# Other written lists of operations for the five engines of an attention and two-layer feed-forward kernel

## The chip, the core and the metric

The kernel runs on one core of a Trainium2 chip. TensorE (PE) multiplies matrices, VectorE (DVE), ScalarE (ACT) and GpSimd (POOL) work elementwise, SyncE (SP) only issues transfers, and 16 DMA engines carry them. PEld is TensorE's weight load, which runs beside its matmuls. The metric is the device time of one launch in microseconds (us), as the median of several runs; lower is better.

## The reference, cut to what matters

```python
# attention: 2 batches x 8 heads, 768 rows of 64; proj is 64 x 6
q_bits = einsum('bhsd,dk->bhsk', q, proj) > 0          # the same for k
mask = q_bucket[..., :, None] == k_bucket[..., None, :]   # 6 bits make a bucket
scores = where(mask, q @ k.T / sqrt(64), -1e9)
attn = exp(scores - scores.max(-1)); attn /= attn.sum(-1) + 1e-9
x = (attn @ v), heads side by side                     # 1536 x 512
# layer 1
h = x @ w_in                                           # 512 -> 2048
x = (h - tanh(h)) @ w_out                              # 2048 -> 512
# layer 2
g = x @ w_gate; val = x @ w_val                        # 512 -> 1536, twice
out = (g * sigmoid(g) * val) @ w_out2                  # 1536 -> 512
```

The weights of the two layers arrive as 64-bit floats and are turned into 32-bit ones on the chip.

## The kernel before, in words

**Attention.** The 16 heads are done as 8 pairs, numbered 0 to 7. A pair is 12 steps (96 in all, steps 0 to 95, so pair 4 begins with step 48): half of the queries, head of the pair, and one of three blocks of 128 query rows. A step is: a score product on PE (four matmuls, L746), a row maximum on DVE (L756), an exponential on ACT (L758), a reciprocal of the sum (L762 and L764), a scaling of the 128x768 block on POOL (L765), six transposes on PE (L776), and two copies out of PSUM on ACT or DVE (L782). Every six steps PE multiplies the transposed block with v (L799).

**Operands of a pair.** For each pair but the first, SP loads both heads of q and of k as 128x768 (L651, into `fs`). Each is split in a high and a low part: the high part by POOL or ACT (L570 or L568), the low part by DVE (L666). The parts are written to the buffers `f` and `q` (high and low part of q) and to the two halves of `raw` (high and low part of k); the names are by turns. From there SP moves them by DMA, SBUF to SBUF, into the operands `op` of the score products: 18 moves for each of seven pairs (L656, 126 in all), 96 KB for a move from `f` or `q` and 192 KB for one from `raw`. A buffer can be written again when the moves out of it have landed, so the split of the next pair waits for the moves of this one. PE also hashes the pair's heads (L709, then bits on DVE, L609, and one-hot products, L743), which DVE and ACT place in the operands (L680, L698). Pair 0 is prepared on its own (L625, L603, L568 to L597) without moves.

**Feed-forward.** From about 241 us PE runs the products of the two layers (L955 and L1009), for which SP loads weights (L371), DVE converts them, and ACT and POOL split them (L385, L387).

**What sets the order.** Every operation has a number, given when it is declared. A planner (`Plan.order`) gives each engine its instructions: the table `ORDER` holds one list of numbers for each of PE, DVE, ACT, POOL and SP, and as long as a list lasts, the engine takes exactly the next number on it. Where an operation may run on two engines, the list in which it stands decides. After its list's end an engine takes the earliest due operation. The program is then written in that order, and on the chip each engine runs its instructions strictly one after the other: one that waits holds up all that stand behind it on that engine. SP is such an engine too, so a move that waits for its source or for its place holds up every later load and move.

Of the kernel before, what the change touches and what calls it, by code (L numbers as in the profile page):

```python
# [46 lines left out]
def chunk_keys():  # L47
# [5 lines left out]
    for i in range(NP2):  # L53
# [11 lines left out]

ORDER = {e: [int(n) for n in t.split()] for e, t in dict(
    PE="""
# [15 lines left out]
    """,  # L83
    DVE="""
# [18 lines left out]
    """,  # L103
    ACT="""
# [15 lines left out]
    """,  # L120
    POOL="""
# [9 lines left out]
    """,  # L131
    SP="""
# [7 lines left out]
    """,  # L140
).items()}

# [1056 lines left out]
```

## Time and profile before

| what | value |
|---|---|
| median of 3 runs | 785.4 us (784.09 to 789.57) |
| the profiled execution | 785.25 us |
| its span, first to last instruction | 783.1 us |
| granted TensorE clock | 1.000 over the span |
| PE busy | 756.5 us (97%) |
| PEld busy | 663.4 us (85%) |
| DVE, ACT, POOL busy | 603.0, 475.5, 333.0 us |

The profiled execution stands 0.15 us under the median. Busy time of PE is counted from modelled ends of pipelined matmuls. A table of stretches (further down) shows where in the span each engine is busy; a wait in brackets behind a row is idle time of that row's engine and what ended it.

### The profile page before, as it was taken

How to read it: one execution, taken by the hardware profiler on the slowest of the kernel's cores; microseconds unless marked ns; L12 is line 12 of the kernel's file. 1: busy time of each engine (PE TensorE's matmuls, PEld its weight loads, DVE VectorE, ACT ScalarE, POOL GpSimd, SP SyncE). 2: the span in 40 equal slices, each digit the busy share in tenths (PEclk: the TensorE clock that was granted, in tenths of full speed). 3: DMA queues.
4: the chain of work that ended last, by engine and by line, in shares of the span. 5: the costliest groups of instructions: out<-in, count | busy, mean ns of one | idle time of the engine just before them, and what ended most of it. 6: DMA issues, size and time to landing. Idle time of an engine off the chain costs nothing.

```text
span 783.1 us, 12379 instructions
## 1 busy us (share of the span) xinstructions
PE 756.5 (97%) x4332; PEld 663.4 (85%) x4332; DVE 603.0 (77%) x1097; ACT 475.5 (61%) x974; POOL 333.0 (43%) x353
## 2 busy tenths in 40 slices
PE   5899999899999999999999999999999999999998
PEld 2667666677678899999999999989998998989996
DVE  4878777668988985988687789898896966777355
ACT  3877777688887664656555656665554554555430
POOL 2655567856776822314232333534332441422120
PEclk9999999999999999999999999999999999999999
DMA  4655361665422132787676671433537657754675
GB/s 128 175 144 152 87 172 40 154 148 159 134 83 82 55 95 65 169 194 196 148 194 151 159 165 57 106 108 109 183 94 177 137 129 156 154 108 75 122 166 197
DMA packets 38717, 104.23 MB, mean 133 GB/s; under 512 B 4704, under 2 KB 10080, under 8 KB 38656
## 3 DMA queue, kind: packets, MB, share of 16 engines
q1 hardware_dynamic: 28288, 71.06, 29.5%
q0 software_dynamic: 9904, 31.59, 23.5%
q10 hardware_dynamic: 464, 0.80, 0.4%
q8 instruction: 34, 0.56, 0.3%
q14 instruction: 27, 0.22, 0.1%
HBM read 49.17 MB, written 18.87 MB: 87 GB/s over the span
## 4 chain that ended last, share of the span: by engine, by line
PE 84%; DMA 7%; DVE 5%; issue 1%; POOL 1%; ACT 1%; SPq 1%; ACTq 0%; DVEq 0%; POOLq 0%
PE bs L955 30%; PE t L1009 15%; PE h L1009 8%; PE s L746 7%; PE x L799 6%; PE t L776 6%; PE x L1009 5%; DMA raw<-in_w 2%; PE x L955 2%; DMA fs<-in_kT 2%; PE t L955 2%; DMA op<-f 1%; DVE m L756 1%; PE h L955 1%; POOL ct L765 1%
## 5 line engine op out<-in xcount | busy, mean ns | idle before, releaser
L955 PE MATMUL bs<-x,wi 128*128 128x384 f32 x1200 | 233.3, 335 | 3.2 <-DVE ct L938 3.2
L955 PEld LDWEIGHTS bs<-x,wi 128*128 128x128 f32 x1200 | 210.3, 188 | 10.5 <-DVE ct L938 5.3
L765 POOL TENSOR_SCALAR ct<-ct,r 128x768 f32<-128x768 f32 x96 | 92.9, 972 | 45.6 <-DVE r L764 31.0
L756 DVE TENSOR_REDUCE m<-s 128x1 f32<-128x768 f32 x96 | 91.1, 952 | 12.7 <-PE s L746 10.5
L746 PE MATMUL s<-op 128*128 128x384 f32 x384 | 94.8, 370 | 2.9 <-ACT ct L758 1.3
L758 ACT ACTIVATE ct<-s,m 128x768 f32<-128x768 f32 x96 | 86.4, 901 | 13.2 <-DVE m L756 9.1
L776 PEld LDWEIGHTS t<-csb,ct 128*128 128x128 f32 x576 | 66.5, 140 | 30.0 <-POOL ct L765 11.2
L776 PE MATMUL t<-csb,ct 128*128 128x128 f32 x576 | 84.2, 276 | 7.9 <-POOL ct L765 6.3
L935 ACT ACTIVATE ct<-bs 128x384 f32<-128x384 f32 x120 | 58.7, 490 | 48.9 <-PE bs L955 48.6
L782 ACT ACTIVATE pt<-t 128x384 f32<-128x384 f32 x129 | 60.6, 489 | 36.9 <-PE t L776 34.8
L746 PEld LDWEIGHTS s<-op 128*128 128x128 f32 x384 | 65.6, 194 | 14.8 <-ACT ct L758 7.0
L1009 PE MATMUL t<-op,wo 128*128 128x384 f32 x384 | 76.5, 335 | 0.0
L799 PE MATMUL x<-pt,v 128*64 128x384 f32 x384 | 69.0, 495 | 0.0
L1009 PEld LDWEIGHTS t<-op,wo 128*128 128x128 f32 x384 | 67.2, 188 | 0.8 <-DVE op L872 0.4
L1009 PE MATMUL t<-wo,op 128*128 128x512 f32 x264 | 67.8, 393 | 0.0
L387 POOL TENSOR_TENSOR wi<-fs,wi 128x512 fp32r<-128x512 f32 (+1 forms) x26 | 40.1, 1544 | 57.0 <-ACT wi L385 56.9
L872 POOL TENSOR_TENSOR ct<-ct 128x384 f32<-128x384 f32 x22 | 23.0, 1045 | 82.4 <-ACT ct L891 62.4
L1009 PEld LDWEIGHTS t<-wo,op 128*128 128x128 f32 x264 | 48.9, 187 | 7.9
L1046 POOL DMA_DIRECT2D acc<-ct x24 | 21.1, 877 | 72.5 <-ACT ct L1038 29.6
L385 ACT ACTIVATE wi<-fs 128x512 fp32r<-128x512 f32 (+1 forms) x60 | 41.8, 701 | 14.1 <-PE bs L955 4.0
L799 PEld LDWEIGHTS x<-pt,v 128*64 128x64 f32 x384 | 24.7, 136 | 28.6 <-issue 28.1
L955 PE MATMUL bs<-op,wi 128*128 128x384 f32 x240 | 47.5, 335 | 0.0
(166 smaller groups left out, 1382.9 us busy)
## 6 DMA issues: line engine op xcount, KB each, us to landing
raw<-in_w SPq DMA_DIRECT2D x68, 512.0 KB, 4.1
acc<-ct POOLq DMA_DIRECT2D x24, 768.0 KB, 6.1
out<-acc POOLq DMA_DIRECT2D x16, 768.0 KB, 7.5
op<-raw SPq DMA_DIRECT2D x42, 192.0 KB, 3.5
op<-f SPq DMA_DIRECT2D x56, 96.0 KB, 3.8
v<-in_v SPq DMA_DIRECT2D x8, 384.0 KB, 4.4
out<-acc SPq DMA_DIRECT2D x4, 768.0 KB, 3.8
acc<-out SPq DMA_DIRECT2D x4, 768.0 KB, 4.4
```

Of the source, the lines that this page charges most:

```text
L385: op({"ACT": act(n)}, lambda e: e.activation(out=hi, in_=src, func=ACTF.Copy), r=rk, w=[wk + (0,)], due=due, late=late)
L387: op({"POOL": pool(n), "DVE": dve(n)}, lambda e: e.tensor_tensor(out=lo, in0=src, in1=hi.bitcast(F32), op=ALU.subtract), r=rk + [wk + (0,) ...
L746: g.matmul(out=s[:, kh, 0:TB], lhsT=(b, a)[first][:, q0], rhs=ks[kh][0 if first else 1], start=first, stop=not first,)
L756: op({"DVE": 0.87}, lambda g: g.tensor_reduce(out=m, in_=sv, axis=AX.XY, op=ALU.max, negate=True), r=[sk + (0,), sk + (1,)], w=[mk])
L758: op({"ACT": 0.9}, lambda g: g.activation(out=p.rearrange("p (a b) -> p a b", a=2), in_=sv, func=ACTF.Exp, bias=m, accum_out=sm), r=[sk + ...
L765: op({"POOL": 0.91}, lambda g: g.tensor_scalar(out=p, in0=p, scalar1=r, scalar2=1.0, op0=ALU.mult, op1=ALU.mult), r=[pk, rk], w=[pk])
L776: g.transpose(out=t_t[z][:, kt * 128:(kt + 1) * 128], in_=p[:, z * TB + kt * 128:z * TB + (kt + 1) * 128], identity=ident)
L782: g.activation(out=dst, in_=src, func=ACTF.Copy) if g is nc.scalar else g.tensor_copy(dst, src),
L799: g.matmul(out=x[r, :], lhsT=v[:, kt, r], rhs=pt_t[ptks[e][1]][:, kt, :], start=(kt == 0), stop=(kt == NKT - 1), tile_position=(0, 64 * e),)
L935: op({"ACT": act(TB)}, lambda e: e.activation(out=dst, in_=bank(), func=ACTF.Copy), r=[bk], w=dk, due=due)
L955: e.matmul(out=bank(), lhsT=w[:, wpart, wi * 256 + k * 128:wi * 256 + k * 128 + 128], rhs=x_at(sb, xn, xpart, k), start=first and m == 0, ...
L1009: e.matmul(out=ps(), lhsT=lhs, rhs=rhs, start=c == 0, stop=c == 5)
```

## The change

The five lists of `ORDER` are other lists. They hold the same operations, and no other line of the kernel differs: the same loads, moves, splits, tiles and buffers. Some 110 operations of the attention stand on another engine than before: 62 of the 192 copies out of PSUM, half of them each way between ACT and DVE, 34 of the small additions (L762) between DVE and POOL, and 15 splits and preparations between ACT and POOL. Of the 14 splits into a high part ACT had three (q of pair 1, k of pairs 2 and 4) and now has five (k of pairs 1 and 7, q of pairs 2, 4 and 7); POOL has the rest. The ends of the lists are alike (PE's from the last steps of the attention on, DVE's and POOL's also), so what moves lies in the attention. Of the diff, the first line of two lists:

```diff
     PE="""
-        13 28 24 20 15 54 64 33 74 40 48 35 44 84 100 102 62 60 112 70 72 135 80 82 145 90 92 157 108 110 167
...
+        13 28 24 20 15 33 54 44 48 64 40 35 74 100 84 62 60 102 72 70 112 135 80 82 145 92 90 157 110 108 167
...
     SP="""
-        5 6 10 9 94 95 123 183 211 127 53 179 181 122 126 261 182 178 207 209 124 128 205 260 177 289 210 293
...
+        5 6 10 9 95 94 53 126 123 128 261 181 179 127 122 124 177 178 206 209 182 183 205 219 289 260 288 211
...
```

Three places show what moves. The first is DVE at the very start, where `bits` is the hash of pair 0's heads (`h` the first, `x` the second head), `m` the row maximum of a step, and `op` the operands. Before:

```order
L579 SCALAR_TENSOR_TENSOR op<-f,op 64x384
L583 TENSOR_SCALAR op<-t,csb 64x384
L756 TENSOR_REDUCE m<-s_116 128x1
L579 SCALAR_TENSOR_TENSOR op<-q,op 64x384
L756 TENSOR_REDUCE m<-s_112 128x1
L609 TENSOR_SCALAR bits<-x 128x384
L594 TENSOR_TENSOR op<-raw,op 64x384 x2
L583 TENSOR_SCALAR op<-h,csb 64x384
L756 TENSOR_REDUCE m<-s_116 128x1
```

and after:

```order
L583 TENSOR_SCALAR op<-t,csb 64x384 x2
L609 TENSOR_SCALAR bits<-x 128x384
L594 TENSOR_TENSOR op<-raw,op 64x384
L756 TENSOR_REDUCE m<-s_116 128x1
L579 SCALAR_TENSOR_TENSOR op<-q,op 64x384
L756 TENSOR_REDUCE m<-s_112 128x1
L583 TENSOR_SCALAR op<-h,csb 64x384
L764 RECIPROCAL r<-r 128x1
L594 TENSOR_TENSOR op<-raw,op 64x384
L756 TENSOR_REDUCE m<-s_116 128x1
```

The second head's bits and one of its two subtractions (L594) now stand ahead of the first maximum, and one split (L579) that stood there is put off. On PE the second head's hash likewise stands ahead of the first score product, where it stood behind the second.

The second place is SP at pair 4's moves and pair 5's loads. Of these rows `raw` is a move of k, `f` and `q` one of the high and of the low part of q, `in_qT` and `in_kT` the loads of pair 5, and `v` the load of v. Before:

```order
L656 DMA op<-raw 64x768
L656 DMA op<-q 64x384
L656 DMA op<-raw 64x768
L656 DMA op<-f 64x384 x2
L656 DMA op<-q 64x384
L656 DMA op<-f 64x384 x3
L787 DMA v<-in_v 128x768
L656 DMA op<-raw 64x768
L651 DMA fs<-in_qT 128x768
L651 DMA fs<-in_kT 128x768
```

and after:

```order
L656 DMA op<-raw 64x768
L787 DMA v<-in_v 128x768
L656 DMA op<-raw 64x768
L656 DMA op<-f 64x384
L656 DMA op<-q 64x384
L656 DMA op<-raw 64x768 x3
L651 DMA fs<-in_kT 128x768
L656 DMA op<-raw 64x768
L656 DMA op<-f 64x384
L656 DMA op<-q 64x384 x2
L651 DMA fs<-in_qT 128x768
```

The move of the low part of q, which stood second, stands behind two moves of k, the load of v and one move of the high part of q; the loads of pair 5 are parted, k's first, behind five of the six moves of k (the sixth follows directly), and q's last.

The third place is POOL at the splits of pair 5, where `raw<-fs` is the high part of k, `f<-fs` that of q, and L765 the scaling of a step. Before:

```order
L570 TENSOR_SCALAR raw<-fs 128x768
L765 TENSOR_SCALAR ct<-ct,r 128x768
L570 TENSOR_SCALAR f<-fs 128x768
L765 TENSOR_SCALAR ct<-ct,r 128x768
L762 TENSOR_SCALAR r<-sm 128x1
```

and after:

```order
L570 TENSOR_SCALAR raw<-fs 128x768
L765 TENSOR_SCALAR ct<-ct,r 128x768
L463 TENSOR_TENSOR x_58<-ct,x_58 128x384
L765 TENSOR_SCALAR ct<-ct,r 128x768 x2
L468 TENSOR_TENSOR ct<-ct 128x384
L765 TENSOR_SCALAR ct<-ct,r 128x768
L468 TENSOR_TENSOR ct<-ct 128x384
L570 TENSOR_SCALAR f<-fs 128x768
```

The split of k stands behind the same scaling as before, the split of q three scalings later.

## Rows read from the trace of the kernel before

**Rows 1.** Busy time in stretches: stretch, its length, then busy us of each engine.

```profile
0.00:22.00 22.00, 12.47 (x51) 6.63 (x52) 11.99 (x24) 9.58 (x17) 6.30 (x15) 1.00 0.44 114
22.00:40.00 18.00, 14.69 (x96) 11.21 (x95) 14.98 (x30) 15.60 (x33) 12.51 (x20) 1.00 0.75 201
40.00:114.00 74.00, 73.16 (x482) 52.09 (x484) 58.56 (x118) 57.94 (x126) 43.40 (x61) 1.00 0.54 141
114.00:122.00 8.00, 4.91 (x32) 3.30 (x30) 3.93 (x6) 3.98 (x9) 6.07 (x7) 1.00 0.13 32
122.00:145.00 23.00, 23.00 (x152) 16.05 (x150) 16.89 (x40) 19.53 (x45) 14.87 (x20) 1.00 0.47 119
145.00:150.00 5.00, 2.90 (x21) 1.77 (x18) 2.11 (x5) 2.19 (x5) 4.57 (x7) 1.00 0.66 128
150.00:241.00 91.00, 90.67 (x586) 63.79 (x585) 77.77 (x160) 72.68 (x158) 63.27 (x78) 1.00 0.44 123
241.00:783.10 542.10, 534.73 (x2928) 508.57 (x2926) 416.79 (x720) 294.05 (x585) 181.98 (x151) 1.00 0.56 134
```

**Rows 2.** Who PE waited for, 22 to 241 us: total, times, longest.

```profile
PE t L776 <- POOL ct L765: 6.3, 7, 1.8
...
PE s L746 <- DMA op<-f: 1.0, 1, 1.0
```

**Rows 3.** POOL in order of time: start, length, instruction, idle before it.

```profile
114.94 0.83 POOL L570 TENSOR_SCALAR raw<-fs 128x768 fp32r<-128x768 f32 x1 [4.15 <-DMA op<-raw]
115.75 0.90 POOL L765 TENSOR_SCALAR ct<-ct,r 128x768 f32<-128x768 f32 x1
117.20 0.95 POOL L570 TENSOR_SCALAR f<-fs 128x768 fp32r<-128x768 f32 x1 [0.54 <-DMA op<-f]
...
144.25 0.83 POOL L570 TENSOR_SCALAR raw<-fs 128x768 fp32r<-128x768 f32 x1 [1.63 <-DMA op<-raw]
```

**Rows 4.** The chain of waits that ended last: start, length, what held.

```profile
35.80 3.83 DMA op<-f
...
105.67 8.40 DMA fs<-in_kT
...
125.25 0.70 PE s L746 x4
...
142.79 4.99 DMA op<-q
```

**Rows 5.** SP's queue in order of time, as it issues transfers.

```profile
87.80 0.46 SPq L656 DMA_DIRECT2D op<-raw  x1
98.84 0.46 SPq L656 DMA_DIRECT2D op<-q  x1
...
114.13 0.61 SPq L656 DMA_DIRECT2D op<-f  x1
133.14 0.46 SPq L656 DMA_DIRECT2D op<-q  x1
```

**Rows 6.** DMA issues: queue, count, size, median us from issue to landing.

```profile
op<-raw SPq DMA_DIRECT2D x42, 192.0 KB, 3.5
```

**Rows 7.** DVE in order of time at the start.

```profile
14.97 0.96 DVE L756 TENSOR_REDUCE m<-s 128x1 f32<-128x768 f32 x1
16.14 0.56 DVE L609 TENSOR_SCALAR bits<-x 128x384 bf16<-128x384 f32 x1 [0.21 <-PE x L625]
16.73 1.02 DVE L594 TENSOR_TENSOR op<-raw,op 64x384 fp32r<-64x384 f32 x2
18.68 0.62 DVE L583 TENSOR_SCALAR op<-h,csb 64x384 fp32r<-64x384 f32 x1 [0.93 <-PE h L603]
19.33 0.96 DVE L756 TENSOR_REDUCE m<-s 128x1 f32<-128x768 f32 x1
...
20.91 0.22 DVE L764 RECIPROCAL r<-r 128x1 f32<-128x1 f32 x2
```

**Rows 8.** DVE in order of time at the splits of pair 6.

```profile
147.89 1.12 DVE L666 SCALAR_TENSOR_TENSOR raw<-fs,raw 128x768 fp32r<-128x768 f32 x1 [3.08 <-DMA op<-q]
```

124 rows, old and new, of tables (ACT, DVE, PE, POOL) are left out of this document.

## The prediction, made blind

> **What bounds the kernel now.** I read the table of stretches first [rows 1]. From 150 us on PE is the bound: it is busy for 90.67 of 91.00 us up to 241 us and for 534.73 of 542.10 us behind that. In the attention it is not busy for 9.53 us of the first 22, 3.31 us of the next 18, 0.84 us from 40 to 114, 3.09 us from 114 to 122, nothing up to 145, and 2.10 us from 145 to 150. The same operations stand in the new lists, so PE's own work stays, and what a new order can give is in these gaps: 9.67 us between 22 and 241 us, and a part of the first 22. Behind 241 us the lists are nearly alike, so I expect the rest to start earlier or later as a whole.
>
> Then who PE waited for [rows 2]: mostly transposes that wait for POOL's scaling, 6.3 us in seven waits, and one score product that waits for a move, 1.0 us. POOL in order of time says why the scaling is late [rows 3]: at 114.94 it starts the split of pair 5's k after 4.15 idle us that a landing move of `raw` ended. It had come there at 110.79 (114.94 - 4.15), and the scalings of the running steps stood behind the split. The split of q at 117.20 waits again, 0.54 us, for a move of `f`. At 144.25 it is the same with pair 6: 1.63 us.
>
> Last, why the moves land late. The chain of waits has a load of k that takes 8.40 us from issue to landing at 105.67, and a move that takes 4.99 us at 142.79 [rows 4], against a median of 3.5 us for the moves of k [rows 6]. SP's queue shows what came ahead of them [rows 5]: it issues a move of pair 4 at 87.80, and nothing more until 98.84, since the next number on its list is a move of a low part that DVE had not made yet. From 98.84 to 114.13 the rest of pair 4, the load of v and both loads of pair 5 go out in one bunch. Then SP stands again until 133.14, for a place of pair 5 that a running step still reads, and a second bunch follows; the split of pair 6 waits for that one.
>
> **The change part by part.**
>
> *Start.* Between the starts of the second maximum, 14.97, and the third, 19.33, DVE spends 4.36 us [rows 7]. In the new list four things stand from the one to the other: the maximum (0.96), the placing L583 (0.62), a reciprocal (0.11, half of two) and one subtraction L594 (0.51, half of two), together 2.20 us; the idle 0.21 and 0.93 us go, because the second head is hashed earlier on PE. That is 2.16 us less. Ahead of the first maximum it adds the bits (0.56) and a subtraction (0.51) and takes away a split of about that size (about the size of the bits), so some 0.5 us more. Net gain 1.65; I take 1.5, since not every idle piece will close. Bounds: 2.16, and nothing, since DVE and ACT are 14.98 and 15.60 of 18.00 us busy in the next stretch [rows 1] and may make the same steps wait there.
>
> *Pair 1.* The move of `f` at 35.80 lands at 39.63 [rows 4], and the first score product of pair 1 waits for it [rows 2]. In the new list it stands in the middle of the pair's moves instead of at their end, ahead of the second load of pair 2. Gain 1.0, the wait; bounds 0 and 1.0.
>
> *Pairs 4 and 5, the main term.* In the new list pair 4's moves of k and of the high part come ahead of the low part on which SP stood idle for 10.6 us (98.84 less the end of the issue before, 88.26), and k's load of pair 5 ahead of q's. So the moves that the split of k needs go out over the idle stretch instead of after it. The split itself stands behind the same scaling as before; the split of q three scalings later, so its 0.54 us fall away too. If the last of the k moves goes out no later than in the old queue and lands in the median 3.5 us, not 8, POOL's 4.15 us shrink to less than 1, and the 3.09 us of PE [rows 1] go. I take 3.1; bounds 0 (the split still waits as long) and 3.1.
>
> *Pair 6's splits.* The first of pair 5's moves in the new list need the places that pair 3's last step reads, a score product that ended at 125.95 (125.25 and 0.70) [rows 4]; before, SP stood until 133.14 [rows 5] on a place that a later step reads. The split of pair 6's k moves behind three further scalings. POOL's 1.63 us [rows 3] and DVE's 3.08 us at 147.89 [rows 8] should go, and PE's 2.10 [rows 1]: gain 2.1; bounds 0 and 2.1.
>
> *Other engines.* The copies that change sides nearly cancel, 31 each way. The added splits on ACT take no more than POOL's 0.83 to 0.95 us [rows 3] and lie beside PE's work, as ACT is busy for 72.68 of 91.00 us at most of the later pairs [rows 1]; nothing for that, unless they wait, which is a rival below.
>
> *New waits.* A list that mends some waits makes others. Upper bound none; I put in one of the length of the wait of pair 1, 1.0 us. The lower bound is that of the slow rival.
>
> Sum: 785.25 - 1.5 - 1.0 - 3.1 - 2.1 + 1.0 = 778.55. The profiled execution stands 0.15 us under the median, which is nothing beside this, so I predict **778.5 us**.
>
> A rule that speaks against the main term: the Trainium skill, DMA: Bandwidth & Descriptors, section Anatomy of one DMA, gives a transfer a fixed cost of about 2.0 us and bytes over 436 GB/s, with nothing for what was issued before it. An estimate from that page for the 384 KB load is 2.9 us; the trace disagrees, with 8.40 [rows 4]. By the page's figure alone the order in the queue would not matter, the terms of pairs 4 and 5 would be nothing, and the sum would be 783.75.
>
> **The rivals.**
>
> *The bunches stay.* All 126 moves and the loads still go through one queue, and every bunch must fit between the last reader of a place and the next pair. For it: the new list still stops on things that steps set free, and the split of pair 5's k still stands directly ahead of a scaling. Against it: the idle 10.6 and 18.4 us of SP (133.14 less 114.74) are there to be used. Then only the start and pair 1 gain, and one new wait comes: 785.25 - 2.5 + 1.0 = 783.75, some 784 us. It also covers that the landings are late for another reason than what stands ahead of them in the queue, and that the gain is given back later, at pair 7 say, whose last moves stand behind loads of weights.
>
> *All gaps close.* A list that avoids the bunches everywhere would also take the rest of the gap from 22 to 40 us, 2.31 us (3.31 less 1.0), the 0.84 and the 0.33 us [rows 1], and make no new wait: 778.55 - 1.0 - 3.48 = 774.07, some 774 us. For it: PE's weight loads are busy for 52.09 of 74.00 us in the attention, where behind 241 us they are for 508.57 of 542.10 [rows 1]. Against it: ACT and DVE are near their own limit from 22 to 40. The Trainium skill, Perfetto Trace Analysis, section Identifying the Most-Contended Engine, holds matmul busy time for a bad metric of headroom and takes the weight loads'; by it there is more to gain in the attention than the gaps of PE's busy time say, which is this rival.
>
> *ACT waits for the landings.* Five high-part splits stand on ACT instead of three. ACT makes the exponentials and most copies out of PSUM, so one that waits there blocks both. If the landing comes more than about 3 us after ACT gets there, as at POOL's 4.15 us, PE loses about 3.1 us at each of five places: 785.25 - 7.7 + 15.5 = 793.05, some 793 us, slower than before. It decides from the third such place on (9.3 against 7.7). Against it: q of pair 2, for one, is split behind the exponential of step 15, and its load is issued long before.
>
> **How the numbers follow.** One per cent, about what a measurement of this kernel can tell from no change, is 7.85 us, so faster begins under 777.5 and slower over 793.3. Chances: the forecast (776 to 781) 0.46, the bunches stay (781 to 788) 0.25, all gaps close (770 to 776) 0.20, ACT waits (788 to 797) 0.09. Faster is the 0.20 and about a third of the forecast, 0.15: 0.35. Slower is about half of the last: 0.05. Within: 0.60. The range from 773 to 787 leaves out about half of the gaps' case, nearly all of the slow one and the end of the bunches, some 0.2. The forecast alone reaches from 776 to 781.
>
> **What would show it.** Right: the third maximum on DVE starts 1 to 2 us earlier; SP issues moves between 89 and 98 us; no load or move near 105 us takes 8 us; PE is busy for over 95% in both stretches, about 108 to 116 and 138 to 143 us in the new time; the first product of the layers (L955) starts near 234 instead of 241 us, and the time behind it stays 542 us. Wrong: POOL's split of k still idles for 3 us or more; SP stands still for 10 us ahead of a bunch; ACT's longest waits name a landing; or the layers take longer by what the attention gained.

## The result, and the profile after

The changed kernel takes 777.38 us (median; 776.99 to 778.23), the kernel before 784.75 us beside it: ratio 0.9895, 95% interval 0.9854 to 0.9937. Run again in the second set of experiments it stood at 0.9902 (0.9889 to 0.9915). The forecast was 778.5 us. The profiled execution takes 777.4 us with a span of 775.6 us, 7.5 us under the span before.

The table of stretches of the changed kernel, cut at its own times (columns as in [rows 1]); PE stretches three to seven lie 6 to 7.5 us earlier than there:

```profile
0.00:22.00 22.00, 13.08 (x60) 7.51 (x61) 12.11 (x24) 10.24 (x19) 7.26 (x17) 1.00 0.57 149
22.00:40.00 18.00, 16.20 (x104) 11.92 (x104) 16.71 (x28) 14.92 (x34) 12.48 (x21) 1.00 0.58 144
40.00:108.00 68.00, 67.99 (x449) 48.40 (x446) 55.86 (x112) 53.11 (x116) 41.00 (x62) 1.00 0.58 148
108.00:116.00 8.00, 8.00 (x56) 5.83 (x55) 7.05 (x15) 6.76 (x15) 5.69 (x6) 1.00 0.50 154
116.00:138.00 22.00, 21.81 (x144) 15.75 (x140) 17.19 (x35) 17.37 (x39) 13.78 (x21) 1.00 0.54 138
138.00:143.00 5.00, 5.00 (x34) 3.41 (x33) 3.12 (x9) 4.57 (x11) 3.23 (x5) 1.00 0.34 102
143.00:233.50 90.50, 89.55 (x581) 62.76 (x580) 77.19 (x158) 75.40 (x165) 68.25 (x79) 1.00 0.42 117
233.50:775.60 542.10, 533.93 (x2921) 507.81 (x2919) 416.81 (x718) 293.25 (x583) 181.20 (x151) 1.00 0.56 134
```

The first product of the layers (L955) starts at 233.0 us, with 542.6 us behind it. PE's idle time (length less the first busy figure) against [rows 1], with the term that the prediction had for it; its new waits had no place in the prediction, and stand here in the last row before the layers:

| stretch | idle before | idle after | gained | forecast |
|---|---|---|---|---|
| first 22 us | 9.53 | 8.92 | 0.61 | 1.5 |
| to 40 us (pair 1) | 3.31 | 1.80 | 1.51 | 1.0 |
| pairs 2, 3 | 0.84 | 0.01 | 0.83 | 0 |
| pairs 4, 5 (two rows) | 3.09 | 0.19 | 2.90 | 3.1 |
| pair 6's splits | 2.10 | 0.00 | 2.10 | 2.1 |
| to the layers | 0.33 | 0.95 | -0.62 | -1.0 |
| layers | 7.37 | 8.17 | -0.80 | 0 |

The sum is 6.53 us. The other 1.0 us of the 7.5 is in PE's busy time, with the same 4332 matmuls; their ends are modelled, so I read it as small waits that they cover, which no run shows.

Who PE waited for in the changed kernel, 22 to 234 us (total, times, longest); the waits for POOL's scaling, 6.3 us in [rows 2], have all but gone, and so has the one for the move of `f`:

```profile
PE s L746 <- ACT ct L758: 1.3, 3, 0.7
PE t L776 <- DVE pt L782: 0.9, 2, 0.5
PE t L776 <- POOL ct L765: 0.5, 2, 0.4
```

Beside those of [rows 2], the kernel before had these, so ACT's have grown and DVE's have not:

```profile
PE t L776 <- DVE pt L782: 1.3, 2, 1.1
PE s L746 <- ACT ct L758: 0.6, 3, 0.3
```

POOL in order of time in the changed kernel: the splits of pair 5's k and q and of pair 6's k, which answer to [rows 3], with no wait for a move in brackets any more:

```profile
107.11 0.84 POOL L570 TENSOR_SCALAR raw<-fs 128x768 fp32r<-128x768 f32 x1
...
117.48 0.84 POOL L570 TENSOR_SCALAR f<-fs 128x768 fp32r<-128x768 f32 x1
...
142.76 0.83 POOL L570 TENSOR_SCALAR raw<-fs 128x768 fp32r<-128x768 f32 x1 [0.25 <-issue]
```

DVE's split of pair 6 stands at 147.06 with no idle ahead, against 3.08 us in [rows 8]:

```profile
147.06 1.01 DVE L666 SCALAR_TENSOR_TENSOR raw<-fs,raw 128x768 fp32r<-128x768 f32 x1
```

SP's queue in the changed kernel, against [rows 5]: it issues between 89 and 98 us, where it had stood, has k's load of pair 5 out at 100.61 instead of 105.67, and stands before pair 5's moves from 111.88 to 119.42 instead of from 114.13 to 133.14:

```profile
92.13 0.46 SPq L656 DMA_DIRECT2D op<-raw  x1
...
98.64 1.88 SPq L656 DMA_DIRECT2D op<-raw  x3
100.61 0.53 SPq L651 DMA_DIRECT2D fs<-in_kT  x1
...
111.88 0.33 SPq L787 DMA_DIRECT2D v<-in_v  x1
119.42 1.75 SPq L656 DMA_DIRECT2D op<-f  x3
```

What the profile says of the two loads of pair 5 (one line for the source L651 between 98 and 125 us) is this in the changed kernel:

```profile
DMA to landing us min/median/max: 4.4/4.8/5.2
```

and this in the kernel before, where the larger is the 8.40 us of [rows 4]:

```profile
DMA to landing us min/median/max: 7.6/8.0/8.4
```

It was not the loads alone. Of the moves (L656 between 98 and 112 us) the slowest took 8.6 us before: a move of `raw` issued at 106.17, which landed at 114.8, just ahead of POOL's split at 114.94 [rows 3]. In the changed kernel the slowest of them took 5.3 us. The line before:

```profile
DMA to landing us min/median/max: 2.0/2.7/8.6
```

and after:

```profile
DMA to landing us min/median/max: 2.0/3.1/5.3
```

The start on DVE, against [rows 7]: the second maximum is at 16.64 instead of 14.97, the third at 18.93 instead of 19.33.

```profile
13.08 0.56 DVE L609 TENSOR_SCALAR bits<-x 128x384 bf16<-128x384 f32 x1 [0.33 <-PE x L625]
13.56 0.54 DVE L594 TENSOR_TENSOR op<-raw,op 64x384 fp32r<-64x384 f32 x1
14.63 0.96 DVE L756 TENSOR_REDUCE m<-s 128x1 f32<-128x768 f32 x1 [0.53 <-PE s L746]
...
16.64 0.96 DVE L756 TENSOR_REDUCE m<-s 128x1 f32<-128x768 f32 x1 [0.47 <-ACT ct L758]
...
18.93 0.96 DVE L756 TENSOR_REDUCE m<-s 128x1 f32<-128x768 f32 x1
```

### The profile page after: what moved, and what is told of

Read it like the earlier page. It is cut to its first block, busy times and chain, and to the rows that moved or that the text cites. A ratio compares the mean times of both kernels' runs of the same rounds, so it can differ in the third digit from the quotient of the medians.

```text
span 775.6 us, 12370 instructions
## 1 busy us (share of the span) xinstructions
PE 755.5 (97%) x4332; PEld 663.4 (86%) x4332; DVE 606.0 (78%) x1092; ACT 475.6 (61%) x975; POOL 332.9 (43%) x357
## 4 chain that ended last, share of the span: by engine, by line
PE 88%; DVE 5%; DMA 3%; ACT 1%; issue 1%; POOL 1%; SPq 0%; ACTq 0%; DVEq 0%; POOLq 0%
PE bs L955 30%; PE t L1009 15%; PE s L746 8%; PE t L776 8%; PE x L799 8%; PE h L1009 8%; PE x L1009 5%; DMA raw<-in_w 2%; PE x L955 2%; PE t L955 2%; DVE m L756 1%; PE h L955 1%; DMA raw<-in_kT 1%; DVE ct L872 1%; PE h L709 1%
## 5 line engine op out<-in xcount | busy, mean ns | idle before, releaser
L955 PE MATMUL bs<-x,wi 128*128 128x384 f32 x1200 | 233.4, 336 | 3.6 <-DVE ct L938 3.6
L955 PEld LDWEIGHTS bs<-x,wi 128*128 128x128 f32 x1200 | 210.4, 188 | 10.8 <-DVE ct L938 5.7
L765 POOL TENSOR_SCALAR ct<-ct,r 128x768 f32<-128x768 f32 x96 | 93.5, 979 | 40.7 <-DVE r L764 28.5
L746 PE MATMUL s<-op 128*128 128x384 f32 x384 | 93.9, 369 | 1.7 <-ACT ct L758 1.5
L746 PEld LDWEIGHTS s<-op 128*128 128x128 f32 x384 | 65.3, 193 | 16.1 <-ACT ct L758 9.8
L387 POOL TENSOR_TENSOR wi<-fs,wi 128x512 fp32r<-128x512 f32 (+1 forms) x27 | 42.1, 1559 | 57.0 <-ACT wi L385 57.0
L955 PE MATMUL bs<-op,wi 128*128 128x384 f32 x240 | 47.5, 335 | 0.0
```

The lines of the kernel that those rows point to most:

```text
L387: op({"POOL": pool(n), "DVE": dve(n)}, lambda e: e.tensor_tensor(out=lo, in0=src, in1=hi.bitcast(F32), op=ALU.subtract), r=rk + [wk + (0,) ...
L746: g.matmul(out=s[:, kh, 0:TB], lhsT=(b, a)[first][:, q0], rhs=ks[kh][0 if first else 1], start=first, stop=not first,)
L765: op({"POOL": 0.91}, lambda g: g.tensor_scalar(out=p, in0=p, scalar1=r, scalar2=1.0, op0=ALU.mult, op1=ALU.mult), r=[pk, rk], w=[pk])
L955: e.matmul(out=bank(), lhsT=w[:, wpart, wi * 256 + k * 128:wi * 256 + k * 128 + 128], rhs=x_at(sb, xn, xpart, k), start=first and m == 0, ...
```

## The experiments

Twelve runs: eleven kernels, each that of before or the changed one with other lists, and the changed kernel once more; the operations are all there in each. The first four write their lists in 15 more lines, so in their rows L761 is L746, L780 is L765, L583 is L568, and so on.

**One engine's list exchanged.** The kernel before with SP's whole new list:

```diff
     SP="""
-        5 6 10 9 94 95 123 183 211 127 53 179 181 122 126 261 182 178 207 209 124 128 205 260 177 289 210 293
...
+        5 6 10 9 95 94 53 126 123 128 261 181 179 127 122 124 177 178 206 209 182 183 205 219 289 260 288 211
...
```

> The kernel before with SP's new list alone; PE, DVE, ACT and POOL keep their old lists. Theory A (the queue: the landings were late because SP stood still on a blocked number and then sent a bunch): the waits at the splits of pairs 5 and 6 go and the move at pair 1 comes in time, 5.2 + 1.0 us, so about 779 us; POOL's idle ahead of the split of pair 5's k falls from 4.15 to under 1.5 us. Theory B (the places: what helped is that the splits stand later on POOL and DVE): SP's list alone gives nothing, about 784 to 785 us.

And the changed kernel with SP's old list, the same lines the other way round:

> The changed kernel with SP's old list alone; the other four keep the new ones. Theory A: the waits of pairs 4 to 6 come back, about 782 to 783 us. Theory B: the splits stand later and still meet their landings, about 777 to 778.5 us.

Measured: 790.85 us, ratio 1.0072 (1.0044 to 1.0099), and 804.68 us, 1.0230 (1.0201 to 1.0259). Both are slower than either parent, which neither theory had. In the first kernel SP's list does what theory A asked of it: POOL's split of pair 5's k starts without a wait, and PE waits for 0.93 us at pair 5 (0.44 and 0.49, at 124.78 and 127.00) and 0.39 us at pair 6 (at 152.13), where it had 3.09 and 2.10. It loses more elsewhere. One row of ACT there; ACT had come to this split at 85.32. The bracket names a move of `f`; the load of k that the split reads was issued at 85.86 and landed after 5.2 us, at 91.06:

```profile
91.14 0.84 ACT L583 ACTIVATE raw<-fs 128x768 fp32r<-128x768 f32 x1 [5.82 <-DMA op<-f]
```

PE behind it:

```profile
92.92 1.65 PE L761 MATMUL s<-op 128*128 128x384 f32 x4 [4.04 <-ACT ct L773]
```

and the stretches there, where the column behind POOL's is the granted clock:

```profile
88.00:94.00 6.00, 1.96 (x10) 1.40 (x7) 0.62 (x2) 2.81 (x5) 0.96 (x2) 0.83 0.72 198
94.00:100.00 6.00, 6.00 (x28) 5.48 (x29) 3.85 (x7) 3.69 (x10) 3.40 (x7) 0.61 0.08 20
```

That is the prediction's slow rival, at one place: a high-part split on ACT waits 5.82 us for a landing, and the exponential behind it keeps PE idle for 4.04 us. At 188.39 PE waits for another 2.70 us, for a scaling. In the second kernel PE waits in long single pieces all through the attention (PE's waits from 22 to 245 us):

```profile
PE t L791 <- POOL ct L780: 15.8, 7, 4.6
PE s L761 <- DMA op<-q: 3.3, 1, 3.3
```

So the new lists of the other engines carry no net gain without SP's, and SP's whole list none without theirs.

**SP's order at pairs 4 and 5 alone**, the 43 transfers from pair 4's first late move to pair 5's last, everything else as before:

```diff
-629 684 633 685 683 712 713 689 711 559 628 774 775 632 687 634 715 630 688 716 717
-884 733 936 807 859 883 802 808 806 803 856 935 885 804 857 888 889 855 860 965 861 887
+683 633 559 629 687 712 630 634 628 775 632 715 716 688 774 711 684 713 717 685 689
+733 861 857 855 802 803 807 806 804 859 856 935 887 885 936 884 808 888 889 883 860 965
```

> The kernel before with SP's new order in the 43 transfers of pairs 4 and 5 alone (the numbers at places 69 to 111 of its list). Theory A: PE's 3.09 and 2.10 us at these two places go, and nothing else, so 779.5 to 780.5 us. Theory B: 784 to 785 us.

**The later splits alone**: pair 5's q (776, and its low part 777 on DVE) behind the scaling of step 43, pair 6's k (939 and 940) behind step 54.

```diff
-        612 642 622 597 652 779 645 777 664 674 686 690 676 655 666 692 667 677 702 718 714 670 735 694 695 745
-        705 737 682 738 755 698 765 708 748 781 783 757 793 758 768 751 795 785 814 786 824 771 796 940 817 789
-        791 836 846 801 838 827 858 862 820 848 839 864 849 886 874 938 890 876 866 896 877 867 906 854 898 899
+        612 642 622 597 652 779 645 664 674 686 690 676 655 666 692 777 667 677 702 718 714 670 735 694 695 745
+        705 737 682 738 755 698 765 708 748 781 783 757 793 758 768 751 795 785 814 786 824 771 796 817 789 791
+        836 846 940 801 838 827 858 862 820 848 839 864 849 886 874 938 890 876 866 896 877 867 906 854 898 899
...
-        593 466 300 585 611 595 621 778 613 776 623 644 646 550 553 556 654 656 678 668 704 552 696 706 747 739
-        749 549 759 767 558 769 939 640 787 816 797 826 818 555 724 727 828 937 840 850 730 868 878 900 910 723
+        593 466 300 585 611 595 621 778 613 623 644 646 550 553 556 654 656 776 678 668 704 552 696 706 747 739
+        749 549 759 767 558 769 640 787 816 797 826 818 939 555 724 727 828 937 840 850 730 868 878 900 910 723
```

> The kernel before with four numbers moved to the places of the new lists: POOL's splits of pair 5's q and pair 6's k behind the scalings of steps 43 and 54, and DVE's splits of the low parts of pair 5's q and pair 6's k behind the maxima of steps 46 and 57; SP's list is the old one. Theory B: the waits go, 780 to 781 us. Theory A: the split of pair 5's k stands where it stood and waits 4 us again, so pair 5 is as before; at pair 6 the later place covers 1.6 to 3 us of waiting: 782.5 to 784 us.

**Both**, the two diffs above together:

> The order before with both edits: the changed order of SP's 43 transfers of pairs 4 and 5, and the four splits behind later scalings. Each alone gave 3 us (3.2 and 2.9). If the two take different waits away (SP's order the late landing ahead of POOL's split of pair 5's k, the moved numbers what stood behind the late ones): the whole 5 us that the changed kernel has less of PE gaps between 114 and 150 us, so 0.9935 to 0.994 of the kernel before. If they are two ways to take away the same wait: 3.2 us again, 0.996, with gaps of about 2 us left there.

**Only pair 4's transfers and pair 5's loads**, the first minus and the first plus line of SP's diff:

> The order before with only the 21 transfers of pair 4 and pair 5's two loads in the changed order. By the prediction's main term the load of pair 5's k then goes out at about 102 us instead of 105.7 and lands in 4 to 5 us instead of 8.4, POOL's split of it no longer idles for 4.15 us, and half to all of the 3.09 us of PE gap between 114 and 122 us goes: 0.996 to 0.998. If the landing was late for another reason than what is issued ahead of it: the split still idles for 3 us or more, and 0.999 to 1.001.

Measured against the kernel before, with PE's idle time of the profiled runs in the three stretches from 114 to 150 us (3.09, 0 and 2.10 us before):

| edit | us | ratio (95%) | idle 114:122, 122:145, 145:150 |
|---|---|---|---|
| SP, pairs 4 and 5 | 782.85 | 0.9962 (0.9948 to 0.9976) | 1.21, 0.54, 0 |
| SP, pair 4 only | 784.49 | 0.9973 (0.9956 to 0.9990) | 1.16, 0.72, 1.11 |
| splits only | 783.18 | 0.9961 (0.9943 to 0.9978) | 1.29, 0.92, 0 |
| SP and splits | 780.83 | 0.9928 (0.9908 to 0.9949) | 0, 0.38, 0 |

SP's order at pair 4 is the mechanism that was forecast: the loads of pair 5 land in 3.9 to 4.9 us in that kernel, against 7.6 and 8.4 before, and the split of k starts without a wait. But the next thing is late. POOL there, in order of time:

```profile
109.58 0.83 POOL L570 TENSOR_SCALAR raw<-fs 128x768 fp32r<-128x768 f32 x1
110.39 0.91 POOL L765 TENSOR_SCALAR ct<-ct,r 128x768 f32<-128x768 f32 x1
113.93 0.84 POOL L570 TENSOR_SCALAR f<-fs 128x768 fp32r<-128x768 f32 x1 [2.62 <-DVE raw L666]
114.75 0.91 POOL L765 TENSOR_SCALAR ct<-ct,r 128x768 f32<-128x768 f32 x1
```

The split of q now idles for 2.62 us with a scaling behind it, so of the 3.09 us 1.16 are still there (0.66 at 115.70 and 0.50 at 117.94) and 1.93 go. Its load was not late, having landed at 111.06 (107.16 and 3.9). The bracket names DVE's low part of k, which ended at 113.85; the last move out of `f`, the buffer that the split writes, landed at about 113.8 (110.9 and 2.9), and no run parts the two. The 0.72 us of the middle column belong to pair 6, since this kernel runs ahead of the one before, and so do the 0.54 us of pairs 4 and 5 together. PE in these two kernels:

```profile
143.39 0.88 PE L776 MATMUL t<-csb,ct 128*128 128x128 f32 x6 [0.68 <-POOL ct L765]
```

```profile
143.66 0.88 PE L791 MATMUL t<-csb,ct 128*128 128x128 f32 x6 [0.53 <-POOL ct L780]
```

With the splits alone it is the other way round; POOL in that kernel:

```profile
113.55 0.83 POOL L585 TENSOR_SCALAR raw<-fs 128x768 fp32r<-128x768 f32 x1 [3.59 <-DMA op<-q]
114.36 2.49 POOL L780 TENSOR_SCALAR ct<-ct,r 128x768 f32<-128x768 f32 x2
```

The split of k waits nearly as long as before, but behind it come two scalings at once instead of one, a split and one. PE still idles for 1.28 us at 115.32, and for 0.92 us at 127.05, behind the split of q in its new place. With both edits the first stretch is full, and so is the last; the first two rows of that kernel:

```profile
114.00:122.00 8.00, 8.00 (x54) 5.49 (x51) 5.08 (x11) 7.15 (x16) 5.36 (x8) 1.00 0.23 63
122.00:145.00 23.00, 22.62 (x152) 16.48 (x151) 17.61 (x39) 19.04 (x42) 15.43 (x21) 1.00 0.55 138
```

At pairs 4 and 5 SP's order takes 1.88 us (3.09 less 1.21), the splits 0.88, and both 2.71, about the sum: each leaves the wait that the other takes. At pair 6 they overlap: the splits alone empty the 2.10 us, and SP's order alone takes 1.56 of them and leaves 0.54. So 3.44 and 2.98 us of idle time make 4.81 together. In time SP's order alone fell short of the 779.5 to 780.5 us that theory A gave it, and the splits alone of theory B's 780 to 781; both together came out as expected.

**The head.** The changed order on all engines up to the scores of step 12, then the order before; of PE's list:

```diff
-        13 28 24 20 15 54 64 33 74 40 48 35 44 84 100 102 62 60 112 70 72 135 80 82 145 90 92 157 108 110 167
-        118 120 185 141 143 130 195 151 153 220 163 165 131 173 175 230 191 240 193 266 201 250 203 268 226 228
+        13 28 24 20 15 33 54 44 48 64 40 35 74 100 84 62 60 102 72 70 112 135 80 82 145 92 90 157 110 108 167
+        120 118 185 143 141 130 151 195 153 220 163 165 131 173 175 230 191 240 193 266 201 250 203 268 226 228
```

> The changed order on all engines up to the scores of step 12 (the first of pair 1), then the order before. Places theory (each stretch gives back its own gaps, and what is won there is kept): the gap of PE shrinks by the 0.61 us up to 22 us and the 1.51 us up to 40 us that the changed kernel shows there, so 2.1 us under the kernel before, ratio 0.9973. Give-back theory (the lead of the head is lost at the next late landing, since the loads and moves of pairs 2 to 5 keep their old order): no difference, ratio 0.999 to 1.001, with PE's gaps between 114 and 150 us longer by what the head won.

And the old order up to there, then the changed one, the same two lines of PE the other way round up to 220:

> The order before on all engines up to the scores of step 12, then the changed order. Places theory: the changed kernel plus 2.1 us, ratio to the kernel before 0.9927 (5.7 us under it), with no PE gap over 1 us between 114 and 150 us. Give-back theory: the changed order takes up a late head, since SP has slack there: within 0.5 us of the changed kernel.

Measured: 782.90 us, 0.9975 (0.9961 to 0.9989), and 778.68 us, 0.9924 (0.9912 to 0.9936). By its ratio the first stands 2.0 us under the kernel before beside them (785.52 us); the second stands 1.6 us over the changed kernel of the same set (777.07). Both sizes agree with the places theory, and what the head wins is kept. The profiled run of the first stands 2.6 us over its median, so its gaps are not set against the others; from 22 to 40 us it idles for 1.81 us, as the changed kernel does (1.80). The second has the changed kernel's full row behind a late head:

```profile
22.00:40.00 18.00, 15.25 (x98) 11.60 (x98) 15.02 (x29) 16.04 (x34) 12.34 (x20) 1.00 0.72 198
40.00:114.00 74.00, 73.99 (x487) 52.15 (x486) 60.48 (x120) 58.16 (x127) 44.52 (x65) 1.00 0.55 144
```

**The four pieces together**, head, SP at pairs 4 and 5 and splits, on the old lists:

> The four pieces that the prediction priced, together and without the rest of the new lists: the changed order up to the scores of step 12, then the order before, with pairs 4 and 5 of SP's list in the changed order and the four splits moved. If these pieces are what the change is worth: 2.0 (the head alone) and 5 us, 0.991, within 1 us of the changed kernel. If the pieces fit only with the lists that they came with (as the joint at step 60 lost 6.5 us): 0.994 or above, with new gaps of PE where one piece runs into a list of before.

Measured: 778.55 us, 0.9905 (0.9886 to 0.9924), the changed kernel's 0.9902 within the interval. Two of its stretches show what is not in the pieces:

```profile
40.00:114.00 74.00, 73.49 (x490) 52.67 (x487) 59.80 (x120) 59.49 (x130) 48.14 (x68) 1.00 0.57 152
150.00:241.00 91.00, 90.66 (x590) 66.87 (x589) 75.15 (x156) 74.40 (x162) 63.80 (x77) 1.00 0.44 124
```

It idles for 0.51 us at pairs 2 and 3, where the changed kernel idles for 0.01, and 0.34 us from 150 to 241 us, as before. The changed kernel wins a little early and gives it back late.

**The late part back.** The changed order up to step 60, then the order before; and a last one with the joint at step 79. Of PE's list in the first:

```diff
-        871 925 879 881 811 903 901 943 913 911 953 923 921 974 891 931 933 984 996 951 949 892 1006 961 959
+        871 869 925 879 881 943 901 903 891 913 911 953 923 921 892 931 974 933 949 984 951 959 996 971 1006
...
```

> The changed order up to the scores of step 60 (pair 5), then the order before on every engine. In the changed kernel the last stretch of the attention lost 0.6 us of PE time (0.33 to 0.93 us) and the layers took 0.8 us longer. If that is the later list: 1.4 us under the changed kernel. If the joint of the two lists costs more than that, or the 1.4 us are not the list's: the changed kernel or 1 to 3 us above it.

> The changed kernel up to the scaling of step 79 (pair 6), and the order before from there, on all engines; SP's list differs in 3 places only. If the 0.6 us of gaps of the last attention stretch and the 0.8 us of the layers come from the changed order there: 1 us under the changed kernel, 0.989. If they don't: 0.9902 as the changed kernel had beside these runs, or a joint that costs 1 us and more.

Measured: 783.60 us, 0.9981 (0.9968 to 0.9994), so 6.5 us over the changed kernel; and 778.08 us, 0.9896 (0.9876 to 0.9916), no difference from it. In the first the joint is what costs, and 6.5 us is more than the 1 to 3 us that were expected of it; POOL there:

```profile
150.00 4.85 POOL L463 TENSOR_TENSOR x<-ct,x 128x384 fp32r<-128x384 f32 x5
154.82 3.13 POOL L468 TENSOR_TENSOR ct<-ct 128x384 f32<-128x384 f32 x3
157.92 2.66 POOL L765 TENSOR_SCALAR ct<-ct,r 128x768 f32<-128x768 f32 x3
```

and PE:

```profile
158.88 1.21 PE L776 MATMUL t<-csb,ct 128*128 128x128 f32 x6 [4.44 <-POOL ct L765]
```

Eight pieces of other work (L463 and L468) fall together ahead of three scalings, and PE idles for 4.44 us. That they meet because one list had put them off and the other does not make room for them is how I read it; no run parts it further. A part of the rest of the 6.5 us is the lower clock behind that pause (last section). The last experiment, and the changed kernel's second profile (first product of the layers at 233.7 us, span 775.6, so 541.9 us of layers against 542.6 in the first; before, 541.8), say that the 0.80 us in the layers' row is not the list's. The 0.62 us ahead of the layers stay open: the list of before from step 79 on does not take them away (it idles for 1.48 us from 150 to 241 us, the changed kernel for 0.93). No version tried beats the changed kernel. It ran once more beside the two head kernels and the first joint:

> The changed kernel once more, beside the other three on the same chip: a ratio of 0.9895 to the kernel before, as in the first runs (7.4 us), or somewhat more if those held a slow run of the kernel before: its profiled span says 7.5 us.

Measured: 777.07 us, 0.9902 (0.9889 to 0.9915); the expected 0.9895 lies in that interval.

## Why the prediction was right, point by point

*Start* (1.5 forecast, 0.61 us of idle time): **mis-sized**. Between the second and the third maximum DVE now spends 2.29 us (18.93 less 16.64) instead of 4.36, 2.07 less, where 2.16 was worked out. What was priced too low is the work put ahead: 0.5 us by DVE's rows. The second maximum comes 1.67 us later, 1.23 us of it already at the first maximum (14.63, before 13.40), since the second head's hash stands ahead of the first score product on PE too. PE in the changed kernel:

```profile
11.51 0.85 PE L625 MATMUL x<-q,pj 64*32 64x384 f32 x2
...
12.95 1.65 PE L746 MATMUL s<-op 128*128 128x384 f32 x4
```

and the first score product before:

```profile
10.92 1.09 PE L746 MATMUL s<-op 128*128 128x384 f32 x2
```

So the third maximum gains 0.40 us, not 1 to 2. I had followed the move on one engine and not on the other.

*Pair 1* (1.0 forecast, 1.51): right, a little small; the wait for the move of `f`, 1.02 us, is gone from PE's waits. The other half comes from waits for POOL up to 40 us, 2.25 us before and 0.35 after, in whose place ACT and DVE keep PE for 1.46 us; the prediction had no term for that. With the start that is 2.1 us for 2.5, and the head alone measured 2.0.

*Pairs 4 and 5* (3.1 forecast, 2.90): the sum is right, the reason about two thirds of it. SP's order does bring the landings forward, and does take POOL's 4.15 us away; alone it is worth 1.9 of the 3.09 us of PE, because the split of q waits next. The later place of that split, which the prediction gave 0.54 us of POOL's time, is the other part: alone it took 0.88 us. A load of k that lands in 8.40 us in one order of the queue and in 4.9 us in another, with 0.9973 (below 1 over its whole interval) for that edit alone, shows that what was issued ahead counts. This disagrees with the 2.9 us that the prediction worked out from the Trainium skill, DMA: Bandwidth & Descriptors, section Anatomy of one DMA; but that section gives its fixed cost and rate for transfers that GpSimd issues, and these loads go out from SP, so it is the use of it here that fails. The 783.75 us beside it leaves out pair 6's 2.1 us as well as the 3.1; without the 3.1 alone the sum is 781.65.

*Pair 6* (2.1 forecast, 2.10): right in size. POOL's and DVE's waits are gone. The prediction gave it to SP's order and named the later place of the split beside it; alone the order takes 1.56 us, and the place all of it.

*New waits* (-1.0 forecast, -0.62 in the row before the layers): right in size; the longest there are 0.36 us for DVE and 0.31 us for ACT.

*Not forecast:* 0.83 us at pairs 2 and 3, 0.80 us the other way in the layers, which comes and goes between runs, and 1.0 us in PE's modelled busy time; together 1.0 us. Another 0.35 us lie outside the span (785.25 less 783.1 is 2.15 us before, 777.4 less 775.6 is 1.8 after). The forecast's own terms come to 6.50 us where 6.7 were worked out, so 0.20 less, and that makes the 1.15 us between 778.55 and 777.4. That the terms come so near is luck in part: the start's 0.89 too little is made up by pair 1 (0.51) and by the new waits (0.38).

*The rivals.* The bunches did not stay. Not all gaps closed: 1.80 us are left up to 40 us and 0.95 before the layers. The rule on weight loads (the Trainium skill, Perfetto Trace Analysis, section Identifying the Most-Contended Engine) was cited for that rival; no run here turns the headroom of PEld, 48.40 of 68.00 us, into time where PE is busy for 67.99. ACT waits for no landing in the changed kernel, but the rival is real: with the two sides' lists mixed it appeared, at more than its forecast 3.1 us for one place.

## What to carry to other kernels

Where a queue in order feeds engines in order, the orders are one schedule: a piece of one list can be worth 3 us at its place, the whole list of one engine, without the others', minus 5 us or worse. Price an engine's wait by what stands behind the waiting instruction: moving the splits behind some scalings gained as much in all as having their data earlier (0.9961 and 0.9962). When work is put ahead of a first step, follow it on every engine that the step passes.

## What the runs showed that I had not expected

A single long pause of PE cost more than its length. In the kernel with SP's new list PE is busy for 1.96 us from 88 to 94 us, and the granted clock of the next 6 us, in which it is busy throughout, is 0.61 on the mean: 0.50, the lower level of 1.2 GHz, up to 98 us, and 1.00, the level of 2.4 GHz, from 100 us on. It ran 28 matmuls there, where the changed kernel runs 56 in a full stretch of 8 us, or 42 in 6; 14 fewer at 7 a microsecond is about 2 us, an estimate from these counts. Six transposes take 1.48 us at 94.36 there, and 0.82 us at 108.94 in the changed kernel.

The other long pauses show the same. In the kernel with the joint at step 60 the clock is 0.72 on the mean from 158 to 164 us, behind the pause of 4.44 us. In the changed kernel with SP's old list, PE's pauses of 4.65, 3.34, 3.22 and 3.40 us are followed by 0.50, 0.66, 0.66 and 0.66 on the mean (40 to 45, 83 to 88, 127 to 132 and 171 to 176 us). So these kernels lose more than the pauses themselves. The kernel before, whose 3.09 us of idle time from 114 to 122 us came in several pieces, showed 1.00 there [rows 1].
